# Six small subtractions of the softmax from GpSimd to VectorE, and a hand-written order rewritten from its 110th step on

## The chip, the cores and the metric

The kernel runs on one core of a Trainium2 chip. The metric is the time on the device in microseconds (us); lower is better. Engines are called PE (TensorE), ACT (ScalarE), DVE (VectorE), POOL (GpSimd) and SP (SyncE, which here issues the transfers).

## The reference

Attention through a memory of 32 slots, for 8 batches of 8 heads, 576 positions and 64 dimensions a head, and behind it a feed-forward layer of 512 by 2048 with a leaky ReLU, over all 4608 positions.

```python
a = phi - np.max(phi, axis=2, keepdims=True)
a = np.exp(a)
a = a / (np.sum(a, axis=2, keepdims=True) + 1e-09)
k_m = np.einsum('bhsm,bhsd->bhmd', a, k)
v_m = np.einsum('bhsm,bhsd->bhmd', a, v)
scores = (1.0 / np.sqrt(q.shape[-1])) * np.matmul(q, k_m.transpose(0, 1, 3, 2))
scores = scores - np.max(scores, axis=-1, keepdims=True)
attn = np.exp(scores)
attn = attn / (np.sum(attn, axis=-1, keepdims=True) + 1e-09)
x = np.matmul(attn, v_m)               # per batch, then (4608, 512)
h = x @ w_in
g = np.maximum(0.01 * h, h)
return g @ w_out
```

## The kernel before

The numbers are float32 in the reference; the kernel splits an operand of a product into a high and a low half in float16 (high = the cast, on ACT; low = value less high, a subtraction) and adds three products. So every matrix operand needs one cast on ACT and one subtraction on DVE or POOL before PE can use it.

A batch b of the attention is a set of steps named `a{b}.…`: loading phi (`a1.phi`), the maximum of phi (`a1.A1`, L655 on DVE) and its spreading by PE (`a1.A2`), the memories `C`, the transposed queries `Q` (L985 on DVE), the scores `E1` (PE, L1043 and L1059), their transposes `E2…` (DVE, L1119), and the softmax `S01` to `S08`, with a second chunk `S11` to `S18` in batches 0 and 1. The last two of these split the result: `S07` casts on ACT (L1200) and `S08` (`S18`) subtracts on POOL (L1205), in two instructions, over 1024 and 128 columns for batches 2 to 7. The scores of batch b are then not multiplied by v: `v_m` is folded into `w_in`, giving weights `W{b}{j}` (`.p` the products, `.h` ACT, `.l` DVE L1279; j is a quarter of the 2048 columns).

The feed-forward layer runs over groups of positions. In the first part (units `u0` to `u7`, and `P8` to `P23` with `V`, `C`, `L`, `O`) each unit has products up (`P`, L1341), the leaky ReLU on ACT (`V`), the cast (`C`, ACT) and the low half (`L`, DVE L1364), and products down (`O`, L1412). Weights are loaded, made into halves and summed on the way: steps `i0` to `i3` (w_in) and `o0` to `o3` (w_out); `o3.l0` and `o3.l1`, for instance, are low halves of sums of w_out (DVE L438), on which the products `O14.0` and `O14.1` wait, and the letter `t` marks steps on L423. `ci.1` to `ci.4` are bounds of w_in; `f01.1` to `f03.2` folds of the first batch.

From about 180 us on the second part runs: 56 quarters k (four to a group), with products up `p{k}.0` to `.3` (PE L1453), the leaky ReLU `v{k}` (ACT L1467, L1469), three sums `s{k}` (DVE L1483 to L1485), casts `c{k}` (ACT L1489), low halves `l{k}` (DVE L1493), and seven products down `d{k}.0` to `.6` (PE L1516), which add up in three PSUM banks and in a part of a fourth. After the fourth quarter of a group G the steps `x{G}.p` and `x{G}.0` to `.3` combine the banks (ACT L1526, DVE L1529, L1531, L1534, L1536) and `z{G}` scales and stores them. The next group's first products `d` write the same banks, in the order in which they are first used: its first product into the third bank waits for `x{G}.3`. So `d4.3`, of the group behind `x3`, waits for `x3.3` in the order before.

The order is written out by hand: two strings of step names, `OPENING` and `LATER`, 2167 tokens in all, run step by step under `tc.manual_schedule`. Each engine takes its instructions in the order in which the steps issue them. Waits between engines follow from the data and the buffers. `far` is true for b >= 2 (`FB` is 2), `NU` is 8.

Of the kernel before, what the change touches and what calls it, by code (L numbers as in the profile page):

```python
# [59 lines left out]
co.2 i0.k1 W00.h1 W00.l0 o0.s0 u7.P1 a1.S07 a2.kv3 W00.l1 co.3 u7.V1 co.4 W10.h0 W10.l0 a1.S08 o0.s1  # L60
a1.S13 a1.S14
# [28 lines left out]
a3.A3 V22.1 O20.0 W21.h0 P23.1 a3.B10 P22.0 i2.l2 L21 a2.S07 W20.h0 O20.1 W20.l0 V22.0 a3.B20 a2.S08  # L90
C22 p0.1 W21.l0 i3.l1 p0.0 i3.l0 O21.0 a3.B3 i3.l2 L22 v0.1 a3.C10 v0.0 W21.h1 V23.1 p0.2 a4.phi
o3.n0 a3.C2 p0.3 P23.0 v0.2 v0.3 O21.1 a3.C30 c0.0 a3.C31 W21.l1 a3.C3k o2.n3 p1.0 a3.q0 v1.0 V23.0
s0 O22.0 p1.2 C23 p1.1 W22.p a4.A1 v1.2 L23 O22.1 v1.1 a3.q1 W22.h1 l0.0 W22.h0 W22.l0 p1.3 v1.3
W22.l1 c0.1 O23.0 p2.0 Z1.0 l0.1 p2.1 a3.C4 W23.p s1 v2.0 O23.1 v2.1 W23.h0 a3.D2 W23.h1 W23.l1 p2.3
W23.l0 a3.Q1 a3.D4 p2.2 c1.0 c1.1 l1.0 d0.0 a3.D11 v2.3 a3.Q0 d0.1 v2.2 a3.D10 p3.1 p3.0 Z2.0 a3.D5
l1.1 d0.5 d0.6 v3.1 v3.0 a3.D6 c2.0 s2 Z2.1 a3.D3 d1.6 p3.3 d1.0 a3.E1 p3.2 d1.1 d0.3 v3.3 d0.2
a3.E23 a3.E22 v3.2 a3.E21 p4.0 W30.p a4.A2 d0.4 c3.0 c2.1 a4.A4 l2.0 a3.E20 l2.1 v4.0 s3 p4.1 p4.2
d2.0 W30.h1 a4.kv v4.2 l3.0 W30.l1 d1.2 d1.3 a4.A3 v4.1 p4.3 d2.3 d3.0 W30.h0 a3.S01 v4.3 p5.0
a3.S02 d2.6 W30.l0 c3.1 l3.1 v5.0 d2.2 p5.1 a3.S03 a4.B10 v5.1 a3.S04 d2.1 d3.3 s4 p5.2 W31.p a4.B20
d3.2 W31.h0 p5.3 d3.1 d1.4 v5.3 d1.5 c4.0 a3.S05 v5.2 W31.h1 l4.0 d2.4 W31.l0 a4.B3 os3 p6.1 c5.0  # L100
# [11 lines left out]
W41.l1 a5.B3 p12.2 d9.1 c11.0 v12.2 a4.S05 v12.3 a5.C10 p13.1 p13.0 s11 d9.2 l11.0 d11.0 W41.h0
c12.0 v13.0 v13.1 a6.phi d11.6 c11.1 a4.S06 p13.3 d9.4 d10.2 z4.0 l11.1 s12 v13.3 a5.C2 p13.2 p14.1
d9.3 d10.4 v13.2 d11.5 c12.1 p14.0 W41.l0 x5.p d10.1 a4.S07 l12.0 l12.1 v14.1 d11.2 v14.0 a5.q0
d11.1 a5.C30 a5.C3k p14.2 c13.0 d10.3 d11.3 d12.0 l13.0 x5.0 a5.q1 x5.1 a5.Q0 a5.D10 v14.2 p14.3
v14.3 d11.4 x5.2 x5.3 s13 d12.1 p15.1 p15.0 d13.0 a5.C31 v15.0 v15.1 d13.1 d12.5 d12.3 a5.D3 a5.Q1
p15.3 z5.0 d12.6 c13.1 p15.2 a6.A1 v15.2 l13.1 d12.4 a5.E1 v15.3 s14 c14.0 p16.0 c15.0 a5.E23 l14.0
p16.1 v16.0 c14.1 a5.E22 v16.1 l15.0 d13.6 a5.C4 d12.2 d13.4 d14.6 d13.5 d13.3 p16.3 l14.1 p16.2
d13.2 d14.2 d15.6 a5.D2 s15 v16.3 a5.E21 v16.2 c15.1 a6.kv p17.0 p17.1 d14.1 v17.0 d15.1 d14.0 c16.0
p17.2 d15.0 a6.A2 a5.D4 v17.1 d14.4 l16.0 z5.1 l15.1 p17.3 a5.E20 d15.2 v17.3 v17.2 c17.0 s16 W42.p  # L120
c16.1 a5.S01 d15.4 p18.0 p18.1 x6.p d14.3 W42.h1 W42.h0 d16.0 W42.l0 v18.0 v18.1 x6.0 d14.5 l16.1
p18.3 p18.2 v18.3 s17 v18.2 l17.0 W43.p d16.5 d15.3 c17.1 x6.1 x6.2 p19.0 a4.S08 l17.1 v19.0 c18.0
# [1607 lines left out]
```

## Time and profile before

| | us |
|---|---|
| median of 3 runs | 648.04 (647.03 to 648.26) |
| the profiled execution | 647.42 |
| its span, first to last instruction | 645.6 |
| PE busy | 633.3 |
| DVE busy | 516.4 |
| ACT busy | 400.1 |
| POOL busy | 35.6 |

The busy times say that PE is the longest queue and that 12 us of the span lie outside its busy time. A row of the trace reads: start, duration, engine, line of the kernel, operation, output and inputs by their names in the program, shapes, how many instructions are put together in the row, and in brackets the idle time of the engine before it with what ended it. Instructions of one engine overlap a little in the trace (some 0.06 us on DVE), so durations in a row add up to slightly more than the time they take.

### The profile page before, as it was taken

The numbers are of one execution on the slowest core, as the hardware profiler recorded it, in microseconds if no ns is written. First come the engines' busy times: TensorE is split into PE (matmuls) and PEld (weight loads), VectorE is DVE, ScalarE is ACT, GpSimd is POOL, SyncE is SP. The second block draws the span as 40 slices with busy tenths as digits, with TensorE's granted clock in tenths as the row PEclk, the third lists the DMA queues.
The fourth block names the chain that finished last, engine by engine and source line by source line (L and its number), as shares of the span: only waits on it lengthen the run. The fifth ranks groups of instructions, "written<-read, shape, count | busy, mean of one in ns | idle before, by whom it ended". The sixth has DMA issues, their size and how long they took to land.

```text
span 645.6 us, 17259 instructions
## 1 busy us (share of the span) xinstructions
PE 633.3 (98%) x7365; PEld 491.5 (76%) x7365; DVE 516.4 (80%) x813; ACT 400.1 (62%) x698; POOL 35.6 (6%) x46
## 2 busy tenths in 40 slices
...
GB/s 322 357 374 258 312 54 33 92 85 32 184 69 87 163 52 63 101 105 92 155 63 1 42 35 76 54 18 182 9 73 36 18 17 17 19 17 19 29 21 50
DMA packets 85404, 61.16 MB, mean 95 GB/s; under 512 B 61648, under 2 KB 68560, under 8 KB 85328
## 3 DMA queue, kind: packets, MB, share of 16 engines
q1 hardware_dynamic: 84752, 59.51, 32.5%
q8 instruction: 58, 0.95, 0.6%
q10 hardware_dynamic: 576, 0.56, 0.3%
q14 instruction: 18, 0.15, 0.1%
...
## 4 chain that ended last, share of the span: by engine, by line
PE 89%; DMA 5%; ACT 1%; DVE 1%; SPq 1%; issue 1%; POOL 0%; DVEq 0%
PE po L1516 34%; PE ph L1453 23%; PE po L1412 13%; PE ph L1341 6%; PE ph L1516 5%; PE pa L1240 4%; PE pa L793 3%; DMA arena<-in_moe_w_in_dram 2%; DMA arena<-in_q_dram 1%; DMA arena<-in_phi_dram 1%; PE pa L1043 1%; DMA wo<-in_k_dram 1%; SPq L620 1%; ACT arena L414 1%; DVE r1k L655 0%
## 5 line engine op out<-in xcount | busy, mean ns | idle before, releaser
L1516 PEld LDWEIGHTS <-arena 128*128 128x128 f16 x2352 | 227.0, 98 | 34.9 <-issue 8.9
L1453 PE MATMUL ph<-a,w_mem 128*128 128x256 f16 (+3 forms) x1512 | 148.3, 245 | 0.0
L1516 PE MATMUL po<-arena 128*128 128x256 f16 x1008 | 129.6, 274 | 2.2 <-DVE obs L1536 2.2
L1516 PE MATMUL po<-wo,arena 128*128 128x256 f16 x1008 | 130.7, 273 | 0.0
L1453 PEld LDWEIGHTS <-w_mem 128*128 128x128 f16 x1512 | 119.7, 98 | 14.3 <-issue 4.2
L1469 ACT ACTIVATE wi<-ph,g_scs 128x256 f32<-128x256 f32 x112 | 53.0, 473 | 88.7 <-PE ph L1453 76.4
L1467 ACT ACTIVATE wi<-ph,g_scs 128x256 f32<-128x256 f32 x112 | 52.9, 472 | 80.8 <-PE ph L1453 77.1
L1412 PE MATMUL po<-wo,arena 128*128 128x512 f16 (+1 forms) x336 | 100.2, 442 | 0.0
L1493 DVE TENSOR_TENSOR arena<-arena 128x1024 f16<-128x1024 f32 x56 | 68.4, 1221 | 32.2 <-ACT arena L1489 31.8
L1489 ACT CAST arena<-arena 128x1024 f16<-128x1024 f32 x56 | 58.4, 1043 | 7.8 <-DVE arena L1485 7.4
L1493 DVE TENSOR_TENSOR arena<-wi,arena 128x768 f16<-128x768 f32 x56 | 53.3, 951 | 12.2 <-ACT arena L1489 12.2
L1205 POOL TENSOR_TENSOR a<-t,a 128x128 f16<-128x128 f32 (+3 forms) x17 | 27.0, 1609 | 443.5 <-ACT a L1200 385.6
L1341 PE MATMUL ph<-a,w_mem 128*128 128x192 f16 (+2 forms) x376 | 48.2, 278 | 0.0
L1489 ACT CAST arena<-wi 128x768 f16<-128x768 f32 x56 | 46.4, 831 | 1.4 <-PE po L1516 0.9
L1483 DVE TENSOR_TENSOR arena<-wi 128x512 f32<-128x512 f32 x56 | 40.3, 719 | 7.7 <-ACT wi L1469 4.5
L1516 PE MATMUL ph<-wo,arena 128*128 128x256 f16 x336 | 45.8, 273 | 0.0
L1412 PEld LDWEIGHTS <-arena 128*128 128x128 f16 x240 | 22.0, 98 | 25.4 <-issue 2.6
L1412 PEld LDWEIGHTS po<-wo,arena 128*128 128x128 f32 x96 | 17.6, 190 | 20.1 <-issue 17.9
L1279 DVE SCALAR_TENSOR_TENSOR w_mem<-pa,w_mem 128x512 f16<-128x512 f32 x40 | 26.9, 680 | 3.7 <-ACT w_mem L1273 3.7
L1240 PE MATMUL pa<-wi,vT 64*32 64x512 f16 (+1 forms) x704 | 28.9, 420 | 0.0
L1273 ACT ACTIVATE w_mem<-pa 128x512 f16<-128x512 f32 x40 | 23.1, 597 | 9.3 <-PE pa L1240 5.2
L1341 PEld LDWEIGHTS <-w_mem 128*128 128x128 f16 x312 | 23.2, 98 | 5.5 <-issue 2.8
...
## 6 DMA issues: line engine op xcount, KB each, us to landing
...
```

The source lines that it names most:

```text
L1205: nc.gpsimd.tensor_tensor(piece(lo, tb), piece(t2, tb), piece(hi, tb), ALU.subtract)
L1240: nc.tensor.matmul(pf[g][cols, :], lhs, rhs, start=(n == 0), stop=(n == len(passes) - 1), tile_position=(g * D, hh * M),)
L1279: nc.vector.scalar_tensor_tensor(tiles(t[:, 1]), w(g), ws, tiles(t[:, 0]), ALU.mult, ALU.subtract)
L1341: nc.tensor.matmul(ph[:, t0:t0 + n], lhs, rhs, start=(m == 0), stop=(m == len(seq) - 1))
L1412: nc.tensor.matmul(po, lhs, rhs, start=(f == 0 and m == 0), stop=(f == NQ * NF - 1 and m == len(seq) - 1),)
L1453: nc.tensor.matmul(ph[:, t0:t0 + n], lhs, rhs, start=(m == 0), stop=(m == len(seq) - 1))
L1467: nc.scalar.activation(dst, ph, AF.Prelu, scale=g_sc2n[:, j:j + 1], alpha=1.0 / SLOPE)
L1469: nc.scalar.activation(dst, ph, AF.Prelu, scale=g_sc2[:, j:j + 1], alpha=SLOPE)
L1483: nc.vector.tensor_tensor(gt[:, 0:2], two, gf[:, 1:3], ALU.subtract)
L1489: nc.scalar.copy(dst[:, 0], src)
L1493: nc.vector.tensor_tensor(dst[:, 1], src, dst[:, 0], ALU.subtract)
L1516: nc.tensor.matmul(acc, g[:, x, s, u], rhs, start=(h == 0 and j == 0 and u == 0 and m == 0), stop=(j == NQ - 1 and u == 1 and m == 2), ski ...
```

## The change

Two edits. First, the low halves of the softmax, `S08`, of batches 2 to 7 are computed on DVE; those of batches 0 and 1 stay on POOL. Second, `OPENING` from its 111th token on and all of `LATER` are replaced by another order of the same 2167 steps. No step is added or taken out, and no product on PE.

```diff
         def chunk(c, b0, b1, f32):
             eng = nc.vector if f32 or b >= FB else nc.gpsimd
+            low_eng = nc.vector if far else nc.gpsimd
...
                 for tb in range(b1 - b0 if b == 1 else 2):
-                    nc.gpsimd.tensor_tensor(
+                    low_eng.tensor_tensor(
                         piece(lo, tb), piece(t2, tb), piece(hi, tb), ALU.subtract
                     )
```

The order, at the places of which the prediction speaks (around `a1.A1`, around `ci.1`, around `O12` to `O15`, around `W20.p`, and around `x3` and `a4.E1`):

```diff
@@ OPENING @@
-u3.P1 u3.P0 i2.h2 i2.y2 o2.h0 a1.phi o2.h1 i2.t0 i2.t2 o2.ld2 u3.V0 o2.y1 f02.1 u2.O0 o2.t0 a1.A1
-a1.kv1 a1.kv0 f02.2 o2.h2 a1.A2 u3.V1 u4.P1 a1.kv2 a1.kv3 a1.A3 o2.t1 a1.B0 a1.B10 i1.b u4.V1 a1.B20
...
-o3.ld1 u4.O0 a2.phi a1.E22 a1.E20 u5.O0 f03.1 a1.S01 a1.E21 ci.1 u4.O1 o3.h2 ci.2 a1.S02 o3.y1 o3.h1
-f03.2 a1.S11 a1.S03 o3.y2 ci.3 a1.S04 o3.ld0 a1.S12 o3.y0 o3.t1 ci.4 u6.P0 e. w1.1 a1.S05 o3.h0
-u7.P0 u6.V0 W10.h1 o3.t0 o3.t2 a2.A1 u6.P1 u7.V0 a2.A2 W00.h0 o3.b a1.S06 u6.O0 u6.V1 W10.l1 co.1
...
+u3.P1 o2.t0 i2.y2 o2.y1 a0.D4 i2.t2 a1.phi o2.ld2 a1.kv1 u1.O1 u3.P0 a0.S16 f02.1 a0.S17 f02.2
+a1.kv0 u3.V0 o2.h2 o2.h1 a1.A1 u2.O0 u3.V1 a1.A2 a1.A3 u4.P1 a1.B0 a1.kv2 a1.kv3 o2.t1 i1.b o2.y2
...
+i3.t0 u5.P0 u5.V0 u4.O0 o3.y2 o3.h2 i3.b u5.O0 a1.E22 f03.1 o3.t2 ci.1 o3.y1 a0.S18 u4.O1 a1.S01
+a1.S11 ci.2 o3.h1 o3.ld0 a1.S02 a1.S03 ci.3 a1.S12 a1.S04 o3.t1 o3.y0 a2.phi f03.2 ci.4 o3.h0 e.
@@ LATER @@
-O11.1 a2.C3k a2.q0 o2.m2 o2.l0 P15.0 o2.n1 o2.s3 a2.C31 o2.l1 V14.1 o2.l2 a1.S18 i1.l2 C14 O12.0 L13
...
-a3.phi P16.0 O13.1 o3.l2 o3.l0 V16.0 o3.k1 a2.C4 o3.s1 P17.0 o3.l1 L15 P17.1 i1.l1 C16 o3.m0 O14.0
-a2.D3 a2.E1 o3.s2 a2.E21 i2.k2 a3.A1 O14.1 V17.1 L16 o3.m3 a2.D2 a2.E22 a2.D4 P18.1 O15.0 V17.0
-o3.m2 O15.1 o3.n2 i2.k1 C17 a2.E3 a2.D11 o3.n3 Z1.1 i2.l0 V18.1 Z1.2 L17 P19.1 P18.0 V18.0 a2.D5
-a2.E20 O16.0 C18 a2.E23 L18 a3.A2 O16.1 V19.1 P19.0 a2.S01 V19.0 a2.S02 P20.1 a2.D6 V20.1 O17.0 C19
-P20.0 O17.1 i2.l1 W20.p V20.0 a2.S03 O18.0 P22.1 a2.S04 P21.0 L19 i3.k0 a2.S05 o3.m1 W20.h1 W20.l1
...
-x3.0 x3.1 p7.0 v6.3 x3.2 d3.6 d3.5 W31.l1 c5.1 p7.1 a4.q0 l5.1 c6.0 d5.0 a4.C3k d4.5 s6 l6.0 a3.S07
-v7.0 a3.S08 d4.1 d4.6 d5.1 p7.2 x3.3 a4.Q0 d5.5 d4.2 c6.1 a4.D10 v7.2 d4.3 v7.1 p7.3 a4.C31 a4.q1
-a4.D3 d5.3 p8.0 d5.2 a4.Q1 d5.6 a4.C4 v7.3 p8.1 v8.1 l6.1 s7 a4.E1 a4.E21 p8.3 a4.E22 c7.0 d4.4
...
+V15.0 O11.1 V14.0 o2.n0 o2.s1 P14.1 o2.l1 o2.m1 o2.l2 a2.D10 a2.D3 a2.Q0 o2.s2 a2.q1 i2.l0 o2.m2
+O12.0 O12.1 V14.1 o2.n1 o2.n2 o3.s0 P15.1 C14 V15.1 o2.s3 o3.s1 o3.k2 a1.S18 a2.Q1 C15 o3.k0 o3.k1
+L14 a2.C4 P16.1 o3.l0 O13.0 o2.m3 L15 O13.1 o3.l2 P16.0 V16.0 a2.E1 V16.1 C16 a2.E20 a2.E22 a3.phi
+o3.s2 P17.0 o3.s3 O14.0 o3.l1 a3.A1 P18.1 V17.0 i3.k0 P17.1 a2.E21 O14.1 o3.m3 o3.m2 a2.E3 V17.1 L16
...
+a2.S01 a2.D5 a2.D6 o3.n1 V18.0 i2.k2 C18 a3.A2 O15.1 a3.A4 Z1.2 L17 P19.0 W20.p a2.S02 Z1.0 V19.1
...
+O20.1 V22.1 P22.0 W21.l0 p0.0 p0.1 o2.n3 a3.B3 v0.0 v0.1 a3.C10 p0.2 p0.3 V22.0 a3.C2 a3.C30 v0.3
...
+p7.0 a3.S07 x3.1 a4.C2 p6.3 x3.2 l5.1 d4.5 d3.6 v7.0 d4.6 v6.3 a4.C30 c6.0 x3.3 W30.l1 l6.0 a4.C3k
+p7.2 p7.1 a3.S08 d4.3 s6 d5.0 a4.Q1 d4.4 v7.1 d4.1 v7.2 p8.0 a4.Q0 p7.3 d5.3 d5.6 v7.3 z3.0 v8.0
+a4.D10 d4.2 d5.2 a4.D3 c6.1 a4.C31 p8.2 a4.E1 a4.C4 d5.1 l6.1 s7 p8.1 v8.1 a5.phi d5.4 d6.0 c7.0
```

## Rows read from the trace of the kernel before

**Rows 1.** Page, part 1: busy time of each engine.

```profile
PE 633.3 (98%) x7365; PEld 491.5 (76%) x7365; DVE 516.4 (80%) x813; ACT 400.1 (62%) x698; POOL 35.6 (6%) x46
```

**Rows 2.** Stretches (us): length, busy PE, PEld, DVE, ACT, POOL, PEclk, DMA share, GB/s.

```profile
60.00:81.00 21.00, 21.00 (x302) 10.65 (x300) 13.92 (x29) 18.04 (x29) 1.50 (x2) 1.00 0.78 264
81.00:162.00 81.00, 80.97 (x735) 47.91 (x735) 79.95 (x134) 63.27 (x104) 9.15 (x7) 1.00 0.25 59
162.00:240.00 78.00, 77.50 (x1140) 57.78 (x1139) 70.73 (x110) 49.21 (x90) 3.50 (x3) 1.00 0.43 111
...
500.00:600.00 100.00, 100.00 (x1110) 88.79 (x1108) 70.50 (x102) 55.99 (x101) 3.52 (x2) 1.00 0.07 17
```

**Rows 3.** PE's waits from 26 us on: total us, times, longest.

```profile
PE po L1516 <- DVE obs L1536: 2.2, 1, 2.2
PE pa L696 <- DVE r1k L655: 1.0, 1, 1.0
```

**Rows 4.** Order of time, 240 to 250 us, all engines.

```profile
241.87 3.61 POOL L1205 TENSOR_TENSOR a<-t,a 128x1024 f16<-128x1024 f32 x2 [59.45 <-ACT a L1200]
...
242.69 2.50 DVE L1483 TENSOR_TENSOR arena<-wi 128x512 f32<-128x512 f32 x1
...
247.74 1.16 PE L1516 MATMUL po<-arena 128*128 128x256 f16 x6 [2.17 <-DVE obs L1536]
```

**Rows 5.** Stretches around that wait, columns as in rows 2.

```profile
44.00:54.00 10.00, 9.00 (x38) 3.88 (x37) 6.71 (x10) 7.76 (x14) 0.00 (x0) 1.00 1.03 394
...
248.00:250.00 2.00, 2.00 (x13) 1.39 (x11) 2.00 (x4) 0.21 (x2) 0.00 (x0) 0.52 0.05 15
250.00:252.00 2.00, 2.00 (x18) 1.59 (x17) 1.86 (x5) 0.00 (x0) 0.00 (x0) 0.63 0.00 0
```

**Rows 6.** POOL's and DVE's groups by form: busy us, mean ns, idle before.

```profile
L1205 POOL TENSOR_TENSOR a<-t,a 128x1024 f16<-128x1024 f32 x6 | 14.6, 2427 | 390.9 <-ACT a L1200 333.0 <-DVE r L827 57.9
L1205 POOL TENSOR_TENSOR a<-t,a 128x128 f16<-128x128 f32 x7 | 6.6, 945 | 0.0
...
L1493 DVE TENSOR_TENSOR arena<-arena 128x1024 f16<-128x1024 f32 x56 | 68.4, 1221 | 32.2 <-ACT arena L1489 31.8
L1493 DVE TENSOR_TENSOR arena<-wi,arena 128x768 f16<-128x768 f32 x56 | 53.3, 951 | 12.2 <-ACT arena L1489 12.2
L1483 DVE TENSOR_TENSOR arena<-wi 128x512 f32<-128x512 f32 x56 | 40.3, 719 | 7.7 <-ACT wi L1469 4.5 <-ACT wi L1467 2.0
L1484 DVE TENSOR_TENSOR arena<-wi,arena 128x256 f32<-128x256 f32 x56 | 23.9, 427 | 1.9
...
L691 DVE TENSOR_TENSOR r1k<-r1k 128x128 f32<-128x128 f32 x6 | 2.2, 364 | 0.0
```

**Rows 7.** Order of time on DVE, one at 78 and one at 303 us.

```profile
78.51 0.28 DVE L493 TENSOR_REDUCE m<-pa 4x1 f32<-4x128 f32 x1 [2.64 <-PE pa L488]
...
305.47 0.96 DVE L1493 TENSOR_TENSOR arena<-wi,arena 128x768 f16<-128x768 f32 x1 [2.04 <-ACT arena L1489]
```

**Rows 8.** Order of time around `a1.A1`, DVE and PE, 47 to 54 us.

```profile
50.73 2.18 DVE L655 TENSOR_REDUCE r1k<-arena 128x128 f32<-128x1152 f32 x1 [1.48 <-DMA arena<-in_phi_dram]
...
53.06 0.30 PE L696 MATMUL pa<-ident,r1k 128*128 128x128 f32 x1 [1.00 <-DVE r1k L655]
```

**Rows 9.** Order of time on DVE, 144 to 160 us: weights for `O14.1` and what follows.

```profile
150.94 1.01 DVE L438 SCALAR_TENSOR_TENSOR wo<-wo,sw,wo 128x768 f16<-128x768 f32 x1
151.87 0.95 DVE L1364 TENSOR_TENSOR arena<-arena 128x768 f16<-128x768 f32 x1
...
153.66 0.69 DVE L458 TENSOR_TENSOR obs<-wo,obs 128x512 f32<-128x512 f32 x1
154.27 0.71 DVE L1119 STREAM_TRANSPOSE t<-pa 128x512 f32<-128x512 f32 x1
```

**Rows 10.** Order of time on PE, 150 to 158 us.

```profile
153.04 2.12 PE L1412 MATMUL po<-wo,arena 128*128 128x512 f16 x9
```

**Rows 11.** POOL in order of time: the pair of batch 4.

```profile
303.45 3.27 POOL L1205 TENSOR_TENSOR a<-t,a 128x1024 f16<-128x1024 f32 x2 [57.90 <-DVE r L827]
```

More of the change, by code (lines that the diff above doesn't have):

```diff
@@ L57 @@
[L57 to L61 removed]
+o0.h0 u1.P1 o1.ld1 u1.V0 o0.y0 a0.S11 u0.P1 i1.y0 o0.t0 i2.ld1 o1.ld2 o0.y1 o0.h1 i1.h2 i1.y2 i1.y1
@@ L62 @@
+W01.l1 a2.A4 a1.S08 u7.V1
 """
@@ L90 @@
[L90 to L100, printed above, removed]
@@ L112 @@
[L112 to L122, printed above, removed]
@@ L140 @@
-d26.6 v29.0 s28 p29.3 os6 c28.1 W52.l1 p29.2 a6.E1 v29.2 d27.2 v29.3 a6.E20 p30.0 p30.1 a6.E21 d27.6
-l28.1 s29 c29.0 d27.4 v30.0 W60.p a6.E22 v30.1 p30.3 a7.A2 x9.p p30.2 W60.h0 x9.0 d27.5 v30.2 a6.E23
-x9.1 a7.A4 d28.0 v30.3 W60.l0 a7.kv c29.1 x9.2 d28.5 x9.3 W53.p W53.h0 l29.0 os5 W53.l0 d28.3 d28.1
-W53.h1 d28.4 W53.l1 d28.6 p31.1 p31.0 v31.0 d29.0 v31.1 d28.2 l29.1 s30 W61.p c30.1 p31.3 p31.2
-a7.A3 c30.0 v31.3 d29.4 d29.6 d29.1 v31.2 l30.0 p32.1 c31.0 l30.1 s31 p32.0 z9.1 z9.0 v32.1 d30.1
@@ new lines @@
+C9 P10.0 V10.1 Z0.0 o0.l0 L9 V10.0 a2.kv1 W12.p P11.0 Z0.2 Z0.1 W12.h0 o0.m2 a2.B10 o1.k1 W12.h1
+P11.1 o0.l2 W12.l0 a1.S15 o0.n2 o1.s0 a1.S16 i1.k2 O8.0 W13.p o1.s1 W03.h1 W12.l1 W03.h0 o1.l1 o1.m0
+a2.kv2 C10 V11.1 W03.l1 L10 O8.1 O9.0 o1.m1 o1.k2 V11.0 W03.l0 i1.l0 P12.1 C11 o1.k0 o1.l2 i2.k0
+P12.0 V12.1 V12.0 o1.l0 o1.n0 O9.1 W13.h0 P13.1 L11 W13.l0 o1.n1 o1.s2 W13.h1 P13.0 O10.0 a2.B20
+V13.1 a2.C10 a1.S17 C12 a2.B3 O10.1 o1.m2 i2.k1 L12 o1.s3 o2.k1 a2.C2 V13.0 i1.l2 o1.n2 o2.k2 o2.s0
+C13 a2.q0 W13.l1 O11.0 a2.C30 a2.C31 o2.m0 i1.l1 P15.0 o2.k0 o1.m3 P14.0 L13 a2.C3k o2.l0 o1.n3
@@ new lines @@
+V19.0 C19 L18 O16.0 P20.1 a2.S03 P20.0 V20.0 W20.h1 V20.1 O16.1 O17.0 C20 O17.1 W20.l1 O18.0 P21.0
+P21.1 L19 i3.k1 L20 W21.p O18.1 V21.0 i3.l0 a2.S04 a3.A3 V21.1 a2.S05 a2.S06 i2.l2 C21 a3.B10 L21
+O19.0 P23.1 P22.1 O19.1 W21.h0 i3.l2 O20.0 a2.S07 a2.S08 W21.h1 W20.h0 i3.l1 a3.B20 W20.l0 V23.1
+O20.1 V22.1 P22.0 W21.l0 p0.0 p0.1 o2.n3 a3.B3 v0.0 v0.1 a3.C10 p0.2 p0.3 V22.0 a3.C2 a3.C30 v0.3
+o3.n0 O21.0 a4.phi P23.0 W21.l1 O21.1 v0.2 s0 p1.0 a3.C3k C22 V23.0 a3.C31 a3.D10 p1.1 a3.C4 L22
+c0.1 C23 a3.q0 l0.1 W22.p O22.0 v1.0 v1.1 L23 c0.0 p1.3 a3.D3 W22.h0 p1.2 O22.1 Z1.1 l0.0 W22.l0
@@ new lines @@
+W23.p v1.2 W22.h1 v1.3 a3.Q0 d0.0 W23.h0 W22.l1 W23.h1 a4.A1 d0.1 p2.0 c1.0 v2.0 O23.0 a4.A2 W23.l1
+os2 a3.q1 p2.1 O23.1 a4.A4 a3.D2 a3.D11 v2.1 s1 p2.2 c1.1 l1.0 p2.3 Z2.0 d1.0 l1.1 d0.3 v2.3 d0.2
+a3.D4 v2.2 Z2.1 W23.l0 p3.1 a3.Q1 a3.D5 a3.D6 d0.5 a4.A3 v3.1 d0.4 s2 p3.0 p3.3 c2.0 a4.B10 a3.E1
+l2.0 v3.3 v3.0 d0.6 a3.E21 a3.E22 c2.1 p3.2 d1.2 d2.0 l2.1 p4.1 W30.p a4.B20 v3.2 d1.1 W30.h0 d1.4
+v4.1 d2.2 p4.3 a3.E20 p4.0 s3 c3.0 W30.h1 l3.0 a3.E23 d1.6 c3.1 a4.kv d1.3 v4.0 W30.l0 p4.2 d2.1
+v4.3 a3.S01 l3.1 W31.p d2.3 p5.1 W31.h0 d3.0 v4.2 a3.S02 v5.1 W31.h1 d2.4 os3 a4.B3 d1.5 p5.0 a3.S03
@@ new lines @@
+c11.1 c11.0 p12.2 a4.S03 d9.6 d9.5 z4.0 v12.3 l11.0 W41.l1 d10.2 d11.0 d10.6 v12.2 d9.4 c12.0 p13.1
+p13.0 v13.1 a4.S04 a5.B3 l11.1 s12 a4.S05 v13.0 a5.C10 p13.2 c12.1 d10.4 p13.3 v13.2 l12.1 d11.4
+x5.p d11.2 a5.C2 d11.1 v13.3 p14.1 a5.q1 p14.0 x5.0 d10.5 l12.0 a5.q0 c13.0 v14.1 d11.6 a6.phi
+a4.S06 d12.0 s13 p14.3 v14.0 d10.3 c13.1 l13.0 d11.3 d12.1 d11.5 x5.1 p14.2 x5.2 a4.S07 x5.3 v14.3
+d12.3 d13.1 v14.2 l13.1 c14.0 s14 d12.2 p15.1 a5.Q0 a5.C30 p15.0 d12.4 a5.Q1 v15.1 v15.0 d13.3 d13.0
+a5.C3k p15.3 p15.2 a5.D10 c14.1 d12.5 v15.3 d13.4 d12.6 l14.1 v15.2 l14.0 s15 a5.C31 z5.0 c15.0
@@ new lines @@
+p16.0 p16.1 a4.S08 l15.0 d13.6 a5.D3 d14.1 c15.1 a5.E1 z5.1 v16.1 a6.A1 a6.A2 v16.0 a5.E22 d13.2
+p16.2 p16.3 v16.3 d14.2 v16.2 d14.0 d14.6 p17.1 p17.0 a5.C4 d13.5 l15.1 s16 a5.E23 a5.D2 d15.6 v17.1
+v17.0 d15.0 p17.3 c16.0 p17.2 c16.1 d15.2 a5.E20 d14.3 x6.p a5.E21 l16.1 d14.4 v17.3 v17.2 d15.1
+p18.1 d14.5 l16.0 p18.0 a5.D4 d15.3 d15.4 c17.0 W42.p x6.0 v18.1 v18.0 p18.2 p18.3 W42.h1 W42.h0 s17
+d15.5 v18.2 x6.1 l17.0 W42.l0 c17.1 d16.0 d16.1 W43.p x6.2 v18.3 p19.1 l17.1 W42.l1 p19.0 d16.3
+d17.1 v19.0 x6.3 W43.h1 s18 p19.2 c18.0 v19.2 v19.1 c18.1 l18.0 l18.1 d17.3 W43.h0 d16.5 d16.4 p20.0
```

163 lines of the change are left out of this document (81 added, 82 removed).

## Prediction

> **What bounds the kernel now.** First the busy times of the engines [rows 1]: PE is busy for 633.3 us of a span of 645.6, POOL for 35.6. The change adds and takes no product, so it can only move the some 12 us in which PE is not busy, and the clock. Then the stretches [rows 2]: from 60 us on PE is dense, and DVE is the engine to watch. From 81 to 162 us it is busy for 79.95 of 81.00 us, so there it is a second bound beside PE; before, from 60 to 81 us, it idles for some 7 us, from 162 to 240 for some 7, and from 500 to 600 us for some 30 (70.50 busy of 100). Then PE's waits from 26 us on [rows 3]: two matter, 2.2 us on DVE's L1536 and 1.0 us on DVE's L655. What comes before 26 us is the same in both orders, as the first 110 tokens are. Last, the places of those two, in order of time [rows 4, 8].
>
> The large wait reads as follows [rows 4]. At 241.87 POOL begins `a3.S08`, 3.61 us long. At 242.69 DVE begins L1483 of `s6`, and it takes 2.50 us, where the mean of the form is 719 ns [rows 6]: 1.78 us too long, while POOL runs. Behind it on DVE stand the rest of `s6`, `l6.0` and `x3.3`, and PE's `d4.3` waits 2.17 us for `x3.3`, as it starts the PSUM bank that `x3.3` empties. Then the granted clock falls: 0.52 from 248 to 250 us and 0.63 from 250 to 252 [rows 5], close to the lower of the two levels for 3.4 us. That loses 2 x 0.48 + 2 x 0.37 = 1.70 us. The place costs 2.17 + 1.70 = 3.87 us.
>
> **The first edit: `S08` of batches 2 to 7 on DVE.** It takes six pairs from POOL, 2427 and 945 ns each, and gives them to DVE. The wide instruction has the form of L1493 with 128x1024, 1221 ns; for the narrow one (128x128, output in float16) no row of DVE is the same: above zero, as it is one more instruction, and below the 364 ns of a float32 subtraction of that size [rows 6]. I take 0.35, as the row is of that shape. A pair costs DVE 1.57 us, all six 9.4. In five batches this lies where PE needs no result of DVE at once: DVE idles for 7 us in 78 at 179 us, and for 30 in 100 in the last part [rows 2]. If that cover is gone (batch 2, at 179 us, has `W20.l0` and with it `p0.0` behind it), the pair costs up to 1.57 us of PE once. And it removes the overlap of POOL and DVE: if all of the 1.78 us at 242.69 comes from POOL, `x3.3` comes 1.78 us sooner less 1.57 for the pair, if the pair stands ahead of it. In the order before, then, the edit alone would gain only 0.2 us of the wait; the order decides the rest.
>
> One rule on such overlaps is weighed here. In the rows L1483 stretched at 242.69, but at 305.47 an L1493, which began while POOL's pair of batch 4 ran to 306.72, took its usual 0.96 us [rows 4, 7, 11]. The Trainium skill ("SBUF — State Buffer", Who interferes with whom) says that a DVE instruction with two SBUF inputs and a GpSimd instruction that reads SBUF exclude each other for a whole instruction, and that the one which issued first wins. The row at 242.69 agrees; the one at 305.47 agrees only if its first POOL instruction had ended. By the rule every pair on POOL may hold DVE for up to 2.4 us, six of them 14.6 us of DVE, against 9.4 for the edit; the sum stays the same, since but one of them reaches PE.
>
> **The second edit: the order around `x3`.** Now `s6`, `l6.0` and `a3.S08` issue behind `x3.3` on DVE, and `s6` behind `a3.S08`. Ahead of `x3.3` DVE has less to do: 0.72 + 2 x 0.43 for `s6` and 0.95 for `l6.0`, 2.5 us, and the stall of 1.78 is not there [rows 4, 6]. 2.17 less 1.78 less 2.5 is below zero by 2.1 us, so `x3.3` ends some 2 us before PE asks for its bank. The wait goes, and with it the fall of the clock: -3.87 us. Next in line are `x3.0` before `d4.5`, by my sums of durations 0.6 to 1.5 us early, and `a4.E1` behind `a4.Q0` and `a4.C31` on DVE, 0 to 0.5 us early (behind `a3.S08`, `s6` and `a4.Q0` there is a queue of 1.57 + 1.57 + 1.37 us on DVE). A wait of 0 to 2 us there; I take 0.4.
>
> **The order around `a1.A1`.** PE waits 1.00 us, as L655 (2.18 us) begins when phi has landed, at 50.73 [rows 8]. In the new order the transfers issue in the same order up to there, and phi may land up to 2 us sooner; but `a0.S16` and more of `o2` stand ahead of `a1.A1` on DVE, and by their durations it begins at 50.3; PE has `u1.O1` and `u3.P0` ahead of `f02.1`, which waits for `i2.t2`, at 49.8 in place of 48.2. So the whole is between 1.0 us less and 1.2 us more; I take +0.45, as `f02.1` is the later of the two.
>
> **The order from 81 to 162 us.** DVE is full here, so each step that is put ahead of another delays it by its duration. `O14.1` starts at 153.04, 1.09 us after `o3.l1` (150.94 + 1.01) [rows 9, 10]. Ahead of `o3.l1` now stand `L15` (0.95), `i1.l1` and `i2.l0` (each of `o3.l1`'s form, 1.01), `o3.s2` (0.69), `a2.E20` (0.71) and `a2.E22` (as the smallest transposes, 0.24): 4.6 us, and 4.24 without the overlaps of 0.06 us. PE has but `P18.1` more ahead of `O14.1`, 12 products, 0.67 us. So 1.09 + 0.67 - 4.24 = -2.5 us: PE would wait 2.5 us. Against that DVE starts earlier: before 81 us it idled for 2.64 us in front of `ci.2` [rows 7], and `o3.t2` (0.7) and `a1.S11` (0.93) are now done in that time. That is a lead of 1.0 to 1.4 us, I take 1.2; and PE comes 0.45 later from the place before. -2.5 + 1.2 + 0.45 = -0.85: a wait of 0.8 us, between 0 and 2.5. Further on `W20.p`, moved 9.7 us ahead on PE, needs `a2.D6`, which moves by 2.1; its margin was 1.7 and DVE idled 1.1 there, so the same wait covers it or adds 0.4. Moved transfers (phi, weights, k and v) meet queues that are filled to 0.25 and 0.43 [rows 2]: no charge; a transfer late by its own length, some us, is the price if that fails.
>
> **After 250 us** DVE idles a third of the time, and by my sums nearly every product has its operand early by over 1 us; `d28.5` behind `x9.2` is the worst, -2.1 us without the idle time of DVE that covers it. 0, at most 1.5.
>
> **The sum.** -3.87 + 0.4 + 0.45 + 0.8 = -2.2 us. The profiled execution took 647.42, its span and 1.8 us around it; it becomes 645.2. It lies 0.62 below the median of the runs, so 645.8 for the median.
>
> A rule that speaks against the change: short waits in place of a long one. In the rows a wait of 1.00 us at 52 left the clock at 1.00, and one of 2.17 us took it down [rows 4, 5, 8]. The Trainium skill ("TensorE: Matmul & The Clock Gate", Part 1) says that the chip halves TensorE's clock after it has been idle and that a kernel of frequent short idles may swing between the two levels. By it the waits of 0.4 to 0.8 us of my sum could cost the clock's 1.7 us too, and the sum would be -0.5; the row at 52 us speaks against that.
>
> **The rivals.**
> - All waits go, the one on L655 too (phi lands sooner, DVE's lead is enough): -3.87 - 1.0 = -4.9, 643.2 us. For it: the idle 2.64 us before `ci.2`. Against it: the sums above are negative at two places. 0.15.
> - No difference: a wait of 2 us forms anew from 240 to 260 us, at `a4.E1` behind the 4.5 us of DVE's queue, or at `x3.0`, and the clock falls as before. Then -3.87 + 2.0 + 1.7 + 0.45 = +0.3, with 0 to -1 for the rest: 647.3 to 648.3. 0.25. The low halves on DVE are what makes it possible.
> - Slower: DVE is the bound from 128 to 160 us. It decides if the lead at 81 us is under 0.3 us: then `O14.1` waits 2.2 us, the clock falls for 1.7, and DVE, behind by as much, is met at 179 us by the pair of batch 2 (1.57) ahead of `W20.l0` and `p0.0`. -3.87 + 0.45 + 2.2 + 1.7 + 1.57 + 0.4 = +2.4, 650.5 us. For it: 79.95 of 81.00 us busy. Against it: `ci.2` and the 7 us idle before. 0.20.
> - The low halves do nothing, the order everything: the same time as the forecast, as the pair is hidden; it is told apart by its own run, not by the time.
>
> **How the numbers follow.** The forecast holds 0.40. What this kernel's measurement can tell from no change is 0.2%, 1.3 us: below 646.7 counts as faster, above 649.3 as slower. Faster: 0.40 + 0.15 = 0.55; the same 0.25; slower 0.20. The range takes in the first rival (643.2) and most of the second and reaches halfway to the third: 643.0 to 649.0.
>
> **What the profile after will show.** POOL's busy time falls by 20 us to 15; no POOL row of the 1024 form; six pairs of 1.22 and 0.35 us more on DVE; no L1483 of over 1 us; no PE wait on L1536 and a clock of 1.00 from 240 to 260 us. Against me would be a wait of PE of over 1.5 us on L438 between 128 and 157 us, one of over 1 us at `a4.E1`, any stretch with a clock under 0.95 after 26 us, or a wait at `a1.A2` of over 2 us.

## The result and the profile after

The changed kernel took 639.66 us (median of 5 runs, 638.94 to 640.91), the kernel before 647.03 in the same call (646.75 to 648.26): a ratio of 0.9882, 95% interval 0.9868 to 0.9896, 7.4 us. Forecast were 645.8 us, a gain of 2.2, and a range that ended at 643.0. The direction was right, the size was not: the gain is more than three times the forecast and the time lies below the range.

The profiled execution of the changed kernel took 639.66 us, 7.76 less than that of before. Its busy times, as in [rows 1]:

```profile
PE 629.6 (99%) x7365; PEld 490.0 (77%) x7365; DVE 518.1 (81%) x825; ACT 402.0 (63%) x698; POOL 12.5 (2%) x34
```

POOL gave 23 us, of which DVE's total shows but 1.7: the 12 instructions cost DVE 8.5 us (1.42 us a pair), and other instructions on it became shorter by some 7. PE's busy time fell by 3.7, though it has the same 7365 products: not all of it is work. PE's waits from 26 us on, as in [rows 3]:

```profile
PE ph L1517 <- DVE t L1119: 0.5, 1, 0.5
PE pa L1087 <- ACT arena L414: 0.2, 1, 0.2
```

Both waits of before are gone, and two small ones are new. The stretches, as in [rows 2, 5]:

```profile
44.00:54.00 10.00, 10.00 (x44) 4.32 (x43) 8.09 (x14) 9.16 (x17) 1.06 (x2) 1.00 1.01 348
...
81.00:162.00 81.00, 81.00 (x768) 48.13 (x768) 79.67 (x135) 66.33 (x108) 4.60 (x8) 1.00 0.33 91
...
240.00:260.00 20.00, 20.00 (x279) 17.57 (x278) 18.11 (x33) 10.43 (x20) 0.10 (x1) 1.00 0.54 141
```

DVE is as full as it was from 81 to 162 us, and PE waits for nothing there; from 240 to 260 us the clock is 1.00. The place of the large wait, as in [rows 4], in order of time on DVE and PE:

```profile
238.03 0.67 DVE L1537 TENSOR_TENSOR obs<-obs,po 128x512 f32<-128x512 f32 x1
...
240.09 1.42 DVE L1206 TENSOR_TENSOR a<-t,a 128x1024 f16<-128x1024 f32 x2
...
241.42 0.68 DVE L1484 TENSOR_TENSOR arena<-wi 128x512 f32<-128x512 f32 x1
241.44 0.82 PE L1517 MATMUL po<-wo,arena 128*128 128x256 f16 x6
```

`x3.3` (L1537) ends at 238.70, 2.7 us before `d4.1` (241.44) asks for its bank; the pair on DVE (L1206) takes 1.42 us, and the sum beside it (L1484) 0.68 in place of 2.50.

Where the 7.3 us between the starts of the last products of the two executions come from, by the intervals from product to product on PE (a loss of before that is gone is negative):

```
wait of d4.3 for x3.3                                   -2.3
low clock behind it                                     -1.7
wait at a1.A2                                           -1.0
gaps in the C10 blocks of batches 4, 6, 7               -2.05   (0.88 + 0.46 + 0.71)
wait in the C10 block of batch 2                        -0.7
new: d16.0 +0.65, a1.E1 +0.4, C10 of batch 1 +0.2       +1.25
many gaps under 0.3 us each                             -0.8
```

The first three lines were known ahead, the next two were not. The last stays open: no run tests it. A `C10` block is 144 small products of one batch in a row (L793), each with its own weight load. In the trace of before and in that of after the block of batch 4 reads:

```profile
230.94 2.23 PE L793 MATMUL pa<-arena 64*32 64x128 f32 x142
...
233.67 0.40 PE L793 MATMUL pa<-arena 64*32 64x128 f32 x2 [0.50 <-issue]
```

```profile
227.35 2.25 PE L793 MATMUL pa<-arena 64*32 64x128 f32 x144
```

The first stopped 2 products before its end, with nothing shown that it waited for ("issue"); the second runs through in 2.25 us.

### The profile page after: what moved, and what is told of

It is laid out like the page before. It is cut to its first block, busy times and chain, and to the rows that moved or that the text cites. A ratio compares the mean times of both kernels' runs of the same rounds, so it can differ in the third digit from the quotient of the medians.

```text
span 637.9 us, 17249 instructions
## 1 busy us (share of the span) xinstructions
PE 629.6 (99%) x7365; PEld 490.0 (77%) x7365; DVE 518.1 (81%) x825; ACT 402.0 (63%) x698; POOL 12.5 (2%) x34
## 4 chain that ended last, share of the span: by engine, by line
PE 90%; DMA 4%; DVE 3%; SPq 2%; issue 1%; ACT 1%; DVEq 0%
PE po L1517 32%; PE ph L1454 22%; PE po L1413 14%; PE ph L1342 7%; PE ph L1517 6%; PE pa L1241 4%; PE pa L793 2%; DMA arena<-in_moe_w_in_dram 2%; SPq L620 2%; DMA arena<-in_q_dram 1%; PE pa L1043 1%; DMA wo<-in_k_dram 1%; DVE arena L1494 1%; DVE r1k L655 0%; PE pa L1087 0%
## 5 line engine op out<-in xcount | busy, mean ns | idle before, releaser
L1454 PE MATMUL ph<-a,w_mem 128*128 128x256 f16 (+3 forms) x1512 | 146.8, 245 | 0.0
L1494 DVE TENSOR_TENSOR arena<-arena 128x1024 f16<-128x1024 f32 x56 | 68.2, 1217 | 20.7 <-ACT arena L1490 20.6
L1494 DVE TENSOR_TENSOR arena<-wi,arena 128x768 f16<-128x768 f32 x56 | 53.3, 952 | 25.5 <-ACT arena L1490 25.2
L1484 DVE TENSOR_TENSOR arena<-wi 128x512 f32<-128x512 f32 x56 | 38.2, 683 | 5.9 <-ACT wi L1468 4.3
L1486 DVE TENSOR_TENSOR arena<-wi,arena 128x256 f32<-128x256 f32 x56 | 23.8, 425 | 1.9
```

What stands on the lines that cost most here:

```text
L1454: nc.tensor.matmul(ph[:, t0:t0 + n], lhs, rhs, start=(m == 0), stop=(m == len(seq) - 1))
L1484: nc.vector.tensor_tensor(gt[:, 0:2], two, gf[:, 1:3], ALU.subtract)
L1486: nc.vector.tensor_tensor(gt[:, 3], gf[:, 3], gt[:, 2], ALU.subtract)
L1494: nc.vector.tensor_tensor(dst[:, 1], src, dst[:, 0], ALU.subtract)
```

## The experiments

Two theories stood against each other on the change itself: A, the order makes the gain and the edit helps little; B, the contention of POOL and DVE cost the time, so the edit makes it. On the gaps in the `C10` blocks: F, TensorE's instructions arrive late; G, something that runs beside the blocks delays them. Unless said otherwise a time is the median, and the ratio is against the kernel before in the same call.

### e1_edit_alone: the low halves on DVE, the order of before

```diff
+            low_eng = nc.vector if far else nc.gpsimd
...
-                    nc.gpsimd.tensor_tensor(
+                    low_eng.tensor_tensor(
```

> The order of before, with the low halves of batches 2 to 7 on VectorE. Theory A (the order removes the wait, the edit only makes it shorter): L1483 in s6 takes 0.7 us in place of 2.50, but the pair a3.S08 now stands ahead of x3.3 on VectorE with 1.4 to 1.6 us, so PE still waits 1.8 to 2.0 us for x3.3; the C10 blocks keep their losses, as no instruction of PE moves; the time is 0 to 0.7 us below before, or 1.7 lower still if the clock does not fall. Theory B (the contention of GpSimd and VectorE is what cost the time, everywhere): the wait goes and with it the fall of the clock, 4 us or more below before.

645.11 us, ratio 0.9970 (0.9955 to 0.9985): 1.9 us below before. The wait stayed (line numbers are one higher here than in before):

```profile
247.86 0.81 PE L1517 MATMUL po<-arena 128*128 128x256 f16 x6 [1.58 <-DVE obs L1537]
```

L1484 took 0.69 us and the pair behind it 1.42, as expected, so `x3.3` came only 0.6 us sooner. The clock did not fall in this execution, and by the mean clock of each run in none of the ten (0.999 to 1.000), where 13 of the 25 runs of before in the same call have 0.997 or less. That is about half of the 1.9 us: the 12 other runs of before have a median of 646.1 us, 1.0 above e1. The edit by itself gives a quarter of the whole gain, half of that as the clock stayed up behind the shorter wait; theory B falls for the whole, but in the old order the edit is not worth nothing.

### e2_order_alone: the new order, the low halves on POOL

```diff
-            low_eng = nc.vector if far else nc.gpsimd
+            low_eng = nc.gpsimd
```

> The new order with all low halves on GpSimd as before. Theory A (the order does it): a pair takes 3.3 us in place of 1.4 and stretches a sum beside it by up to 1.8 us, but x3.3 stands ahead of it; p0.0, which has 2.3 us after the end of a2.S08, waits 0 to 1 us: 0 to 2 us above the changed kernel (639.7 to 641.7). Theory B (the contention cost the time): the gain is gone, 645 us or more.

640.96 us, ratio 0.9918 (0.9893 to 0.9942): 6.0 us below before, 1.3 above the changed kernel, with intervals that overlap. Theory A holds, and more sharply than the medians say: from the first `C10` block to the last product the traces of e2 and of the changed kernel take 575.75 and 575.74 us. They differ ahead of that block, which begins at 58.99 and 57.90 us, while the first pair that the edit moves comes at 175 us. So in the new order no gain of the edit is seen. And yet the contention is there, in all six pairs. The pair of batch 4 on POOL, and the low half beside it on DVE:

```profile
302.81 3.49 POOL L1206 TENSOR_TENSOR a<-t,a 128x1024 f16<-128x1024 f32 x2 [62.66 <-PE po L1517]
```

```profile
303.42 2.60 DVE L1494 TENSOR_TENSOR arena<-arena 128x1024 f16<-128x1024 f32 x1
...
306.12 0.73 DVE L1484 TENSOR_TENSOR arena<-wi 128x512 f32<-128x512 f32 x1
```

L1494 took 2.60 us in place of 1.22: it ends at 306.02, behind POOL's first instruction (302.81 to 304.94 in the records) by its own 1.1 to 1.2 us. In five of the pairs one instruction of DVE takes 0.7 to 1.9 us more than the median of its form, in the sixth 0.4. PE hardly sees it: from 81 us on it has two waits, of 0.3 and 0.2 us. That nothing which PE needs at once stands behind these places in the new order is a reading of it, not tested by itself.

### e3_old_shift and e4_new_shift: 60 more instructions at TensorE's start

```diff
         for _ in range(n):
+            if f32 and len(cut) < 5:
+                cut.append(1)
+                for x in range(NF):
+                    nc.tensor.matmul(idle_sums[0][:, x], by, ones, start=True, stop=True)
+                continue
             nc.tensor.matmul(idle_sums[0], by, of, start=True, stop=True)
```

The products split here are those that only keep PE busy while the first loads run; their result is not used.

What theory F was formed from: the profile's queue "q8 instruction" moved 58 pieces, 0.95 MB, so 16 KB each; PE's 14,796 instructions (7365 products, 7365 weight loads, 66 waits) are 255 a piece. The start of each `C10` block in TensorE's stream, modulo 256, and what the block took over the 1.98 us of an undisturbed one (from its first product to the start of its last):

```
            batch 2    batch 3    batch 4    batch 5    batch 6    batch 7
before     247: 0.67*  24: 0.00  166: 0.88   23: 0.00  201: 0.46  174: 0.71
after      232: 0.00   14: 0.00  131: 0.00  106: 0.00  234: 0.00  218: 0.00
old_shift   51: 0.70*  84: 0.00  226: 0.00   83: 0.00    5: 0.00  234: 0.00
new_shift   36: 0.00   74: 0.00  191: 0.34  166: 0.78   38: 0.00   22: 0.00
* at the block's start, behind DVE's L1279
```

> The kernel before, with five of the idle products at its start split in four, which puts 60 more instructions into TensorE's stream ahead of everything that is of interest, and changes no order. Theory F (the gaps in the C10 blocks are TensorE's instructions arriving late: they are fetched in pieces of 256, and a block of 288 instructions in 1.98 us that begins at 166 to 201 of a piece runs dry): the blocks of batches 4, 6 and 7 move from 166, 201 and 174 to 226, 5 and 234 and lose nothing in place of 0.88, 0.46 and 0.71 us: 2.05 us below before; the 0.67 us of batch 2, which is of another kind, stays. Theory G (the gaps come from what runs beside the blocks): 0.

> The changed kernel with the same 60 instructions more at its start. Theory F: the blocks of batches 4 and 5 move from 131 and 106 to 191 and 166, where before lost 0.46 to 0.88 us, and lose about 0.56 and 0.88; all others stay free of loss: 1.45 us above the changed kernel, 641.1. Theory G: no difference, 639.7.

The kernel before with the shift: 645.75 us, ratio 0.9974 (0.9957 to 0.9990), 1.2 us below before; all three losses are gone, as the table has it, and 0.7 us came back as a new wait of PE for `x3.1`, as PE now was sooner at the same DVE:

```profile
PE po L1516 <- DVE obs L1536: 2.3, 1, 2.3
PE po L1516 <- DVE obs L1531: 0.7, 1, 0.7
```

The changed kernel with the shift: 640.25 us, 0.6 above the changed kernel, where 1.45 were expected. The two were measured in different calls and their intervals overlap; from the first `C10` block to the last product the traces take 576.40 and 575.74 us. What decides is the blocks. The losses appeared in the two blocks that were named ahead, 0.34 and 0.78 us for the 0.56 and 0.88 expected, and in no other. The block of batch 5, undisturbed in all other kernels here:

```profile
289.17 2.23 PE L793 MATMUL pa<-arena 64*32 64x128 f32 x142
291.79 0.40 PE L793 MATMUL pa<-arena 64*32 64x128 f32 x2 [0.39 <-issue]
```

Nothing beside the blocks was changed. Theory G falls. The traces show one thing more that G can't explain: in all 14 blocks with such a loss, in five kernels, the block stops behind the same instruction of the stream, number 192 modulo 256, wherever it began (in before behind 142, 124 and 138 of its 144 products). In each of them a transfer of q8 begins within 0.4 us of the block's start (-0.32, -0.06 and +0.30 us in before), and the block goes on 2.3 to 2.9 us after that. The 256 instructions of a piece last but 1.76 us in such a block (256 of 288, in 1.98 us). That the next piece is asked for too late is inferred from these times; no record shows the request.

### e5_old_x3_first: only the wait at x3.3

```diff
-d4.5 s6 l6.0 a3.S07 v7.0 a3.S08 d4.1 d4.6 d5.1 p7.2 x3.3 a4.Q0
+d4.5 a3.S07 v7.0 d4.1 d4.6 d5.1 p7.2 x3.3 s6 l6.0 a3.S08 a4.Q0
```

> The order of before and its engines; only s6, l6.0 and a3.S08 are moved behind x3.3. Theory A: x3.3 now follows l5.1 on VectorE at once, its bank is free some 3 us before d4.3 wants it, the wait of 2.17 us and the fall of the clock (1.70) go, though GpSimd still runs its pair and s6 is still stretched, behind x3.3: 3.9 us below before. Rival: the stretched s6 moves the wait to the next that needs VectorE, a4.E1 or d6: 0 to 2 us below before.

645.39 us, ratio 0.9975 (0.9961 to 0.9988): 2.3 us below before where 3.9 were expected. The wait for `x3.3` went, and another took its place (line numbers are one lower in this kernel):

```profile
242.32 2.02 DVE L1482 TENSOR_TENSOR arena<-wi 128x512 f32<-128x512 f32 x1
...
245.40 1.04 ACT L1488 CAST arena<-arena 128x1024 f16<-128x1024 f32 x1 [3.89 <-DVE arena L1484]
...
247.24 0.81 PE L1452 MATMUL ph<-a,w_mem 128*128 128x256 f16 x6 [1.86 <-ACT wi L1466]
```

DVE's first sum of `s6` is still stretched (2.02 us) by POOL; ACT stands idle for 3.89 us in front of the cast `c6.1`, which needs `s6`, with the leaky ReLU of the next quarter queued behind it; and PE waits 1.86 us for that ReLU. So the place had two walls one behind the other, one on DVE and one through ACT. And most of what was gained is the clock: it stayed up in all ten runs (mean 0.999 or more), where 13 of the 19 runs of before in this call have 0.997 or less; the other six have a median of 646.2 us, 0.8 above e5.

### e6_new_till_A3: only the start of the new order

The first 198 steps of the new order, then the rest in the old one.

> The new order for the first 198 steps (to a1.A3, 52 us), then what is left in the order of before, low halves on GpSimd. Theory: i1.y0 and i1.t0 earlier let o1.ld0 issue 2 us earlier, the full queue of transfers delivers phi of batch 1 at 47.8 in place of 50.7 us, and the wait of 1.0 us at a1.A2 goes; everything behind keeps its waits, the 2.2 us at x3.3 and the losses in the C10 blocks of batches 4, 6 and 7: 0.8 to 1.2 us below before. Rival: the next stretch (VectorE, full from 81 us on) takes it back at O12 to O14: 0 to 0.3 below.

646.54 us, ratio 0.9984 (0.9970 to 0.9999): 1.2 us below before, as expected, though the time shows little: the interval reaches from 0.1 to 1.9 us, and 5 of its 10 runs have a mean clock of 0.997 or less, for 13 of 19 of before. The wait at `a1.A2` is not among PE's waits any more; the two large ones of the rest are those of before (line numbers one lower):

```profile
PE po L1515 <- DVE obs L1535: 2.2, 1, 2.2
PE pa L792 <- issue: 0.8, 2, 0.5
PE pa L1058 <- ACT w_mem L1608: 0.3, 1, 0.3
```

In this execution the wait of 2.2 us did not take the clock down (columns as in [rows 2]):

```profile
248.00:250.00 2.00, 2.00 (x26) 1.86 (x25) 1.98 (x5) 0.23 (x1) 0.00 (x0) 1.00 0.03 8
250.00:252.00 2.00, 2.00 (x47) 1.79 (x52) 1.78 (x4) 0.49 (x2) 0.00 (x0) 1.00 0.00 0
```

### e7_three_parts and e9_three_parts_and_edit: the parts together

e7: e6's start, e5's move and the 60 instructions, low halves on POOL. e9: the same with the edit of e1.

> The order of before with three changes: the first 198 steps of the new order, x3.3 ahead of s6, l6.0 and a3.S08, and 60 more instructions at TensorE's start; low halves on GpSimd. If the three account for the gain and add up: 1.0 + 3.87 + 2.05 = 6.9 us below before, 640.1; what e3_old_shift gave back (0.7 us in a new wait at x3.1) may be lost here too, 640.8. If the gain needs the whole new order: 643 or more.

> e7_three_parts with the low halves of batches 2 to 7 on VectorE as well. Theory: in e7 the wait at x3.3 was replaced by one of 2.0 us on ScalarE: the cast c6.1 stood behind s6, which GpSimd's pair stretched by 1.4 us, and the leaky ReLU that PE needs stood behind c6.1. Without the pair on GpSimd s6 takes 1.6 us and ends 1.4 us sooner: PE waits 0.4 to 0.6 us there, and the time is 1.4 us below e7_three_parts, 642.8 (4.4 to 5 below before). Rival: the pair on VectorE itself (1.4 us) delays something else by as much, and nothing is gained: 644.2.

e7: 644.18 us, ratio 0.9946 (0.9928 to 0.9965), 3.5 us below before, half of the 6.9 that the parts were to add up to, and in the range that was put down for "the gain needs the whole new order"; e3, e5 and e6, each alone, had given 1.2, 2.3 and 1.2. e9: 642.12 us, ratio 0.9918 (0.9900 to 0.9935), 4.9 below, 2.1 less than e7. PE's waits in e7 (line numbers one lower), then in e9:

```profile
PE ph L1452 <- ACT wi L1466: 2.0, 1, 2.0
PE po L1515 <- DVE obs L1530: 0.7, 1, 0.7
PE pa L1058 <- ACT w_mem L1608: 0.2, 1, 0.2
```

```profile
PE ph L1453 <- ACT wi L1467: 0.6, 1, 0.6
PE po L1516 <- DVE obs L1536: 0.4, 1, 0.4
PE pa L1058 <- ACT w_mem L1609: 0.3, 1, 0.3
```

The wait through ACT fell from 2.0 to 0.6 us with the pair off POOL, as was said ahead. So in this order the edit pays where `s6` stands in front of `c6.1`. From e9 to the changed kernel in the same call (e11, below) 2.2 us are left; these three waits, 1.3 us, and the 0.7 us in the `C10` block of batch 2, which e9 still has, are of that size.

### e8_new_more_dve: 1.2 us more on DVE ahead of o3.l1

```diff
+    def extra():
+        nc.vector.tensor_reduce(
+            sm.tile([P, 1], F32, name="m1"), ones.unsqueeze(1).broadcast_to([P, 2 * NF, P]),
+            AX.XY, ALU.max
+        )
...
-... O14.0 o3.l1 a3.A1 P18.1 ...
+... O14.0 extra o3.l1 a3.A1 P18.1 ...
```

> The changed kernel with one more instruction on VectorE, a maximum over 1024 columns of a constant, some 1.2 us, ahead of o3.l1. Theory: VectorE is a second bound up to there without any slack (o3.l1 ends at 152.37, O14.1 begins at 152.28): PE waits 1.0 to 1.2 us for it, and the time is 0.9 to 1.2 above the changed kernel, 640.7. Rival: there is slack left, 0 to 0.3 above.

640.87 us, 1.2 above the changed kernel of another call, with intervals that overlap; from the first `C10` block to the last product the trace takes 576.37 us for 575.74. The instruction took 1.21 us, and `O14.1` waited:

```profile
153.40 1.89 PE L1413 MATMUL po<-wo,arena 128*128 128x512 f16 x8 [0.89 <-DVE wo L438]
```

DVE is a second bound up to this place with 0.3 us to spare (1.21 less 0.89).

### e10_new_two_moves and e11_new_again: can the new waits go?

```diff
-... s16 a5.E23 a5.D2 ...
+... a5.E22 a5.E23 d13.2 ...
...
-a1.D5 a1.D4 a1.D10 a1.D3 a1.Q0 i3.h0
+a1.D5 a1.Q0 a1.D4 a1.D10 a1.D3 i3.h0
```

> The changed kernel with two moves on VectorE: a5.E23 (0.24 us) from behind s16 to behind a5.E22, as d16.0 waits 0.65 us for it, and a1.Q0 ahead of a1.D4, as a1.E1 waits 0.4 us for it. Theory: both waits go, 1.0 us below the changed kernel of the same call. Rival: the next operand is as late (the low halves l16, the loads of q), 0 to 0.3 below.

> The changed kernel itself, to compare the other two with on the same chip: 639.0 to 640.9; the C10 blocks of batches 2 to 7 without loss again, a wait of 0.5 us at 321 us, a clock of 1.00 from 26 us to the end of the products.

e11: 639.88 us (638.55 to 641.95), ratio 0.9889 (0.9869 to 0.9909). Its `C10` blocks of batches 2 to 7 lose nothing, the wait at `d16.0` is there with 0.3 us, and another, of 0.7 us at 34.8 us on DVE's L423, was not expected. e10: 641.04 (639.20 to 641.75), ratio 0.9905 (0.9887 to 0.9922): not below e11. The wait at `a1.E1` is not listed any more, the other moved with the instruction:

```profile
317.77 0.82 PE L1517 MATMUL ph<-wo,arena 128*128 128x256 f16 x6 [0.53 <-DVE t L1119]
```

Six executions of the new opening (after, e2, e4, e8, e10, e11) reach the first `C10` block at 57.90, 58.99, 57.71, 57.67, 57.97 and 58.94 us, four of the old one (before, e1, e3, e5) at 60.31, 60.98, 59.60 and 59.33: while the loads run, an execution differs from the next by over 1 us, which hides a gain of this size. From that block to the last product the trace of e10 takes 575.29 us, 0.4 less than that of e11 (575.66), 0.3 of it ahead of the block of batch 2, where `a1.E1` lies.

## Why the prediction was wrong

Of the 7.4 us the sum had 2.2. Its large term held. Two steps failed. The bound at its start, by which nothing but the idle 12 us of PE and the clock can move, left out the gaps in the `C10` blocks. And the three waits that the new order was to bring, 1.65 us together, did not come, while the wait at `a1.A2` went; other waits, of 1.25 us, came where none was forecast.

**The order around x3: right, with its size.** `x3.3` was to end some 2 us before its bank is wanted; it ends 2.7 before. The wait and the fall of the clock went, L1483's 2.50 us became 0.68, and a pair costs DVE 1.42 us for the 1.57 forecast. That the 1.70 us of the clock belong to the wait was taken as certain; in e6 the same wait left the clock at 1.00, in before and e3 it did not. e1 confirms the statement that the edit alone leaves the wait (1.58 us for the 1.96 of the working), but not that it gains only 0.2 us, as the clock stayed up. The rival by which the low halves do nothing and the order everything is borne out by e2.

**Missed: the gaps in the C10 blocks, 2.05 us.** They stood in the trace of before as PE waiting for "issue", as the third line of the same list of waits from which [rows 3] has the first two:

```profile
PE pa L793 <- issue: 0.8, 2, 0.5
```

The prediction went by the two lines that name an engine. The view put down but part of each gap, and the rest counted as PE busy. The statement at the start of the prediction, that a change without a product added or taken can only move the 12 us in which PE is not busy, and the clock, was a step that failed: PE's busy time fell by 3.7 us, of which 1.7 are the clock and some 2 gaps in `C10` blocks that the view counts as busy.

**Missed: the wait in the C10 block of batch 2, 0.7 us**, on DVE, which in the trace of before stands on the weight load (PEld), not on the product:

```profile
128.74 2.24 PEld L793 LDWEIGHTS pa<-arena 64*32 64x32 f32 x142 [0.28 <-DVE w_mem L1279]
```

It is in every kernel here with the old order at that place and in none with the new one; no run moved it by itself.

**The start: wrong sign, 1.0 us gained for 0.45 lost.** That phi lands sooner was right (47.8 for 50.7 us). That `f02.1` would wait for `i2.t2` to 49.8 us was not: DVE ran `i2.t2` at 47.38, as before (47.49), and `f02.1` began at 48.27 (48.17 before). The sum of durations ahead of it had put DVE's work in line without the idle time that it replaces. The wait itself was not a fixed 1.0 us: in the other three executions of the old opening (e1, e3, e5) it was 0.8, 0.5 and 0.3 us, and in none of the nine that begin with the new one is it listed.

```profile
48.49 2.17 DVE L655 TENSOR_REDUCE r1k<-arena 128x128 f32<-128x1152 f32 x1
...
51.97 0.27 PE L696 MATMUL pa<-ident,r1k 128*128 128x128 f32 x1
```

In order of time in after, DVE and PE: `a1.A1` ends at 50.66, and PE comes to `a1.A2` 1.3 us later without a wait [rows 8].

**From 81 to 162 us: 0.8 us forecast, none came.** `o3.l1` was to move by 4.24 less 1.2 us on DVE and moved by 0.42, from 150.94 to 151.36 [rows 9]:

```profile
151.36 1.01 DVE L438 SCALAR_TENSOR_TENSOR wo<-wo,sw,wo 128x768 f16<-128x768 f32 x1
```

The same instructions became shorter. In before two sums of L458 beside POOL's pair of batch 1, and a small L1154 (L1155 in after) beside POOL's L1144, read, in order of time on DVE:

```profile
80.74 1.09 DVE L1154 TENSOR_SCALAR ts__836<-ts__836 128x12 f32<-128x12 f32 x1
...
123.23 1.40 DVE L458 TENSOR_TENSOR arena<-wo,arena 128x512 f32<-128x512 f32 x1
124.67 1.29 DVE L458 TENSOR_TENSOR arena<-wo 128x512 f32<-128x512 f32 x1
```

In after they read:

```profile
79.30 0.17 DVE L1155 TENSOR_SCALAR ts__836<-ts__836 128x12 f32<-128x12 f32 x1
...
123.75 0.68 DVE L458 TENSOR_TENSOR arena<-wo,arena 128x512 f32<-128x512 f32 x1
...
127.36 0.67 DVE L458 TENSOR_TENSOR arena<-wo 128x512 f32<-128x512 f32 x1
```

These three and a few smaller ones (two of L511 took 0.52 and 0.61 us in before and 0.17 in after) give DVE 2.8 us ahead of `O14.1`: steps of batches 0 and 1, which stay on POOL, but which the new order puts beside other work of DVE. That is read from what overlaps in the two traces; no run moved these steps alone. The prediction said that of the overlaps but one reaches PE; it weighed only those of the edit. The rule of the Trainium skill that was cited ("SBUF — State Buffer", Who interferes with whom), and by which an overlap can cost DVE the whole of POOL's instruction, agrees with e2 (L1494 at 2.60 us); the row at 305.47 that seemed to speak against it does not, as POOL's first instruction ended at 305.58 in the records, 0.11 us after it began. The other rule cited from the Trainium skill ("TensorE: Matmul & The Clock Gate", Part 1), by which short idles may make the clock swing, is not borne out: no profiled execution of the new order lost the clock between 26 us and the last products, and the ten runs of the changed kernel in its two calls have a mean clock of 0.999 or 1.000. One of the ten runs of e2, at 0.997 and 646.98 us, may have lost it.

**The term for 160 to 250 us** (0.4 us at `a4.E1`) did not come; after 250 us 0 was forecast and 0.65 came, at `d16.0`, which no step named. The waits of the sum that were put on at +0.45, +0.8 and +0.4 were sums of durations on one engine against another; they were off by 1.45, 0.8 and 0.4 us, all on the side of a loss. The rival in which all waits go (643.2) was nearer and lacked mainly the gaps.
